# A layer norm, a Hedgehog attention and a SwiGLU on one core: fourteen more matmul instructions for the same columns

## The chip, the cores and the metric

The kernel runs on 1 core of one Trainium2 chip. The metric is the device time of one execution in microseconds (us); where several runs are shown, their median counts. A profile of one execution comes with the runs. Its span is the time from the first to the last instruction of the program; the time of that execution is a little longer than its span.

## The reference, cut to what matters

```python
x = A_x                                   # 1 x 2048 x 640, bf16
xn = _layernorm(x, axis=-1)
return x + _A_ref(xn, A_wqkv, A_w_phi, A_wo) + _B_ref(xn, B_w1, B_w3, B_w2)

def _A_ref(x, wqkv, w_phi, wo):           # 32 heads of 20
    q, k, v = ...                         # x @ wqkv
    phi_q = concat(softmax(q @ w_phi), softmax(-(q @ w_phi)))
    phi_k = concat(softmax(k @ w_phi), softmax(-(k @ w_phi)))
    kv, z = phi_k.T @ v, phi_k.sum(s)
    return ((phi_q @ kv) / (phi_q @ z + 1e-6)) @ wo

def _B_ref(x, w1, w3, w2):                # F = 1536
    return (silu(x @ w1) * (x @ w3)) @ w2
```

## The kernel before

The 2048 tokens are 16 tiles of 128. The order of the work is written out by hand, engine by engine; no planner moves anything, and each engine runs its own list in order. SyncE (SP in the profile) issues all DMAs from one queue.

**Start.** The first tiles of x and parts of the weights are loaded. Until they are there, TensorE multiplies zeros into a bank of PSUM that nobody reads: `warm(n, cols)` (L219 to L221) issues n such idle matmuls of `cols` columns. At the start stand two matmuls of 128 columns and `warm(2 * WARM, P // 2)`, 40 of 64 columns (L223 to L226). Then TensorE transposes tile 0 of x (`by_pe`, L294), runs `warm(4)` (four idle matmuls of 128 columns, L766), and transposes tile 1. Layer norm statistics, V products of the raw tiles (`raw_part`, L306), further transposes by DMA (`by_dma`, L758) and the first SwiGLU units (`glu_half`, L473) follow. The loads of the SwiGLU weights w1 and w3 stand in the same SP queue as the transposes.

**K stage.** For each tile: the fused K projection (`phi_unit`, L411), softmax features, the running sum of phi_k times v (`kv_unit`, L496), and SwiGLU units as filler.

**Q stage** (the loop at L935). For each of the 16 tiles t: the fused Q projection, its softmax features, a transpose of them by DMA, two tiles later the attention product (`r_unit`, L530) and the transpose of its result. For t from 0 to 6 two SwiGLU units fill TensorE: a unit (`glu_unit`, L454; `fill`, L706) has five matmuls of 512 columns for the gate and five for the up product, one for each 128 rows of the weights. `fill_halves(gate, up)` (L710) is the same unit with the last `gate` and `up` of the five matmuls cut into two matmuls of 256 columns with the same weights. Before, at t = 0, it is called as `fill_halves(2, 2)`; all other units are whole. Later turns of the loop compute the output: three groups of four tiles transposed (`out_piece`, L646) and four tiles directly (`out_unit`, L590).

**End.** The last tile's result is computed in three parts of 384, 160 and 96 columns; the first two parts are added and the first is stored. Then every engine comes to a branch (L998): a flag computed on the way says whether the fast softmax without maximum was safe. Where it was not, a general path repeats everything in loops (two loops, 86 matmuls in their bodies). Where it was, as with these inputs, every engine jumps over the general path's code to a short part in which VectorE adds the last 96 columns and SP stores the rest of the tile. On TensorE this code that is jumped over has 335 instructions in the assembled program; nothing is left for TensorE behind it but the closing barrier (L1048). Every matmul of the program is two TensorE instructions, a weight load (PEld) and the product (PE).

```python
        finish = res
        with tc.If(ok == 0) as general:
            ...
        with general.Else():
            nc.vector.memset(drift[:, 0:1], 0.0)
            finish()
```

Of the kernel before, what the change touches and what calls it, by code (L numbers as in the profile page):

```python
# [8 lines left out]
P = 128  # L9
# [3 lines left out]
def kernel(  # L13
# [53 lines left out]
    def bank(name, dt=f32):  # L67
        n = 512 if dt == f32 else 1024
        return psum.tile([P, n], dt, name=name, tag="bank")
# [75 lines left out]
    def ld(dst, src):  # L145
        nc.sync.dma_start(out=dst, in_=src)
# [9 lines left out]
    with tc.manual_schedule():  # L156
# [62 lines left out]
        def warm(n, cols=P):  # L219
            for _ in range(n):  # L220
                nc.tensor.matmul(idle[:, 0:cols], nought[:], nought[:, 0:cols])  # L221
# [19 lines left out]
        def ln_stats(*ts):  # L241
            made = []
            for t in ts:
                xt = xin[:, (t // 4) % 3, t % 4, :]
                st = work.tile([P, 2, 6], f32, name="st")
                for i in range(2):
                    nc.vector.bn_stats(out=st[:, i, :], in_=xt[:, i * HD : (i + 1) * HD])  # L247
                made.append(st)
            for t, st in zip(ts, made):
                nc.vector.bn_aggr(out=mv[:, t, :], in_=st[:])  # L250
# [43 lines left out]
        def by_pe(dst, t, ps):  # L294
            xt = xin[:, (t // 4) % 3, t % 4, :]
            for c in range(KD):
                nc.tensor.transpose(  # L297
                    ps[:, c * P : (c + 1) * P], xt[:, c * P : (c + 1) * P], ident[:]
                )
            for c0, c1 in ((0, 2), (2, KD)):  # L300
                nc.scalar.copy(  # L301
                    out=dst[:, c0:c1, t * P : (t + 1) * P],
                    in_=ps[:, c0 * P : c1 * P].rearrange("p (c s) -> p c s", s=P),
                )
# [43 lines left out]
        def tile_of(t):  # L348
            return slice(t * P, (t + 1) * P)
# [61 lines left out]
        def phi_unit(t, w, name, exps=exps, cols=None):  # L411

            ps = by_token(cols or tile_of(t), w, name, CH)
            dst = phi[:, t % 4]
            exps(ps, dst)
            rows = dst.rearrange("p c g f -> p (c g) f")[:, :, 0:60].rearrange(
                "p a (i d) -> p a i d", d=Dh
            )
            sk = work.tile([P, 2 * NCH, 3], f32, name="sk")
            nc.vector.reduce_sum(out=sk[:], in_=rows, axis=AX.X)  # L420
            rk = work.tile([P, 2 * NCH, 3], f32, name="rk")
            nc.vector.reciprocal(out=rk[:], in_=sk[:])  # L422
            nc.gpsimd.tensor_mul(  # L423
                out=rows, in0=rows, in1=rk[:, :, :, None].to_broadcast([P, 2 * NCH, 3, Dh])
            )
# [28 lines left out]
        def glu_unit(sc, fi, banks=None):  # L454

            gp, up = banks or (bank("gp")[:], bank("up")[:])
            for ps, w in ((gp, w1), (up, w3)):
                for c in range(KD):
                    nc.tensor.matmul(  # L459
                        ps,  # L460
                        w[:, c, fi * P : (fi + 1) * P],
                        xnT[:, c, sc * 512 : (sc + 1) * 512],
                        start=(c == 0),
                        stop=(c == KD - 1),
                    )
            return glu_done(sc, fi, gp, up)

        def glu_done(sc, fi, gp, up):
            th = work.tile([P, 512], f32, name="th")
            nc.scalar.activation(out=th[:], in_=gp, func=AF.Tanh, scale=0.5)  # L470
            return lambda: glu_product(sc, fi, gp, up, th)
# [24 lines left out]
        def kv_unit(t, v1, acc, first, last):  # L496

            for c in range(NCH):
                b, i = divmod(c, 6)
                nc.tensor.matmul(  # L500
                    acc[:, b, VC * i : VC * i + 1 + Dh * HC[c]],
                    phi[:, t % 4, c].rearrange("p g f -> p (g f)"),
                    v1[:, c, 0 : 1 + Dh * HC[c]],
                    start=(first and i == 0),
                    stop=last,
                    skip_group_check=True,
                )
# [77 lines left out]
        def residual(rows):  # L585
            xr = work.tile([P, D], bf, name="xr")
            ld(xr[:], x2[rows, :])
            return xr
# [83 lines left out]
        def group_stored(g, i):  # L672
            rows = out2[(4 * g + 2 * i) * P : (4 * g + 2 * i + 2) * P, :]
            ld(
                rows.rearrange("(t p) d -> p t d", p=P),
                y[:, 2 * i : 2 * i + 2].rearrange("p t c s -> p t (c s)"),
            )
# [28 lines left out]
        def fill(n):  # L706
            for _ in range(n):
                glu_unit(*glu.pop(0))()

        def fill_halves(gate, up):  # L710

            sc, fi = glu.pop(0)
            gp, upp = bank("gp")[:], bank("up")[:]
            for ps, w, whole in ((gp, w1, KD - gate), (upp, w3, KD - up)):
                for c in range(KD):
                    n = 1 if c < whole else 2
                    for i in range(n):
                        a, b = i * 512 // n, (i + 1) * 512 // n
                        nc.tensor.matmul(
                            ps[:, a:b],  # L720
                            w[:, c, fi * P : (fi + 1) * P],
                            xnT[:, c, sc * 512 + a : sc * 512 + b],
                            start=(c == 0),
                            stop=(c == KD - 1),
                            skip_group_check=True,
                        )
            glu_done(sc, fi, gp, upp)()
# [35 lines left out]

        pst = [bank("pst", bf), bank("pst", bf)]
        by_pe(xrT, 0, pst[0])
        warm(4)  # L766
        ln_stats(0)
        ln_root(0)
        by_pe(xrT, 1, pst[1])
# [165 lines left out]
        for t in range(NST + 4):  # L935
            if t < NST:
                phi_unit(t, wqphi, "pq")
            if t < 2:
                kv_unit(turns[t - 2], vaug[:, turns[t - 2]], acc, False, t == 1)
                if t == 1:  # L940
                    kv_done([acc[:, 0], acc[:, 1]])
                    ld(w2, B_w2.rearrange("(c p) d -> p c d", p=P))
            if t < 7:
                (fill_halves(2, 2) if t == 0 else fill(1))
                fill(1)
            for g, c in pieces.get(t, []):
                out_piece(g, c)
            outs = {16: (12,), 19: (13, 14, 15)}.get(t, ())
            for j in outs:
                last = tile_of(j) if j == NST - 1 else None  # L950
                res = out_unit(hT[:, j], tile_of(j % 4), xrs[j], last)
                if j == 13:
                    group_stored(2, 0)
                    group_stored(2, 1)
                if 13 <= j < 15:
                    xrs[j + 1] = residual(tile_of(j + 1))
                if last is None:
                    ld(out2[tile_of(j), :], res[:])
            if 2 <= t < NST + 2:
                r_unit(t - 2)  # L960
            if t < NST:
                phi_transposed(t)
            if 2 <= t < NST + 2:
                o_transposed(t - 2, (t - 2) // 4)
            if t in backs:
                group_back(*backs[t])
            if t in (12, 13):
                group_stored(0, t - 12)
            if t == 17:
                group_stored(1, 0)  # L970
            if 2 <= t < 6:
                x_back(t - 2)
            if 7 <= t < 11:
                x_back(t - 3)
            if 13 <= t < 17:
                x_back(t - 5)
            if t == 15:
                xrs[12] = residual(tile_of(12))
            if t == 17:
                xrs[13] = residual(tile_of(13))  # L980
            if t == 18:
                group_stored(1, 1)
                group_back(2, 0)
                group_back(2, 1)
            if t < 4:
                norm_unit(wqphi, 1, t)
            if t == 4:
                ld(listed[:], norms[:])
                ld(flat, listed[:].rearrange("p g -> (p g)").partition_broadcast(1))
            if t == 10:  # L990
                flag_unit()
            if t == 12:
                ok = nc.values_load(flag[0:1, 0:1], min_val=0, max_val=1)
# [59 lines left out]
```

## Time and profile before

| what | value |
|---|---|
| runs shown | 268.24, 268.84, 269.27 us; median 268.84 |
| the profiled execution's own time | 268.56 us |
| its span | 266.9 us |
| TensorE (PE) busy | 261.0 us, 98% of the span, 1854 matmuls recorded |
| weight loads (PEld) recorded | 1880 |
| VectorE, ScalarE, GpSimd busy | 72%, 42%, 34% |
| DMA | 31.41 MB, 118 GB/s in the mean |

The profile's page lists busy time by engine, the span in 40 slices, DMA queues, the chain of work that ended last, and the costliest groups of instructions; other views of the same trace answer for a window, a line or an engine. A small share of matmul records is missing from a trace: 26 of 1880 here, as each weight load has one matmul. An engine's name with a q (PEldq, SPq) is its sequencer: it waits, branches or issues DMAs, and is not counted as busy. The DMA queues named "instruction" carry the program's code to the engines.

### The profile page before, as it was taken

How to read it: one execution, taken by the hardware profiler on the slowest of the kernel's cores; microseconds unless marked ns; L12 is line 12 of the kernel's file. 1: busy time of each engine (PE TensorE's matmuls, PEld its weight loads, DVE VectorE, ACT ScalarE, POOL GpSimd, SP SyncE). 2: the span in 40 equal slices, each digit the busy share in tenths (PEclk: the TensorE clock that was granted, in tenths of full speed). 3: DMA queues.
4: the chain of work that ended last, by engine and by line, in shares of the span. 5: the costliest groups of instructions: out<-in, count | busy, mean ns of one | idle time of the engine just before them, and what ended most of it. 6: DMA issues, size and time to landing. Idle time of an engine off the chain costs nothing.

```text
span 266.9 us, 5027 instructions
## 1 busy us (share of the span) xinstructions
PE 261.0 (98%) x1854; PEld 153.2 (57%) x1880; DVE 193.3 (72%) x356; ACT 113.0 (42%) x347; POOL 90.7 (34%) x83
## 2 busy tenths in 40 slices
PE   8999999999999999999999999999999999999994
PEld 7766475655556555555655555555555555644663
DVE  4899973397876877799888999999699866125121
ACT  5764344746567753366766554423322330000000
POOL 5022620055544444443373333336434543000000
PEclk9999999999999999999999999999999999999999
DMA  6997866976000001500008855563768789552871
GB/s 190 234 259 168 119 122 144 366 133 122 1 2 0 1 3 8 167 2 0 2 0 251 180 120 116 93 133 89 130 153 97 165 200 159 128 116 47 221 209 55
DMA packets 83484, 31.41 MB, mean 118 GB/s; under 512 B 71935, under 2 KB 82047, under 8 KB 83456
## 3 DMA queue, kind: packets, MB, share of 16 engines
q1 hardware_dynamic: 83456, 31.05, 53.5%
q8 instruction: 16, 0.26, 0.4%
q14 instruction: 12, 0.10, 0.1%
HBM read 11.17 MB, written 2.63 MB: 52 GB/s over the span
## 4 chain that ended last, share of the span: by engine, by line
PE 94%; DMA 2%; ACT 1%; issue 1%; SPq 0%; DVE 0%
PE up L459 18%; PE gp L459 18%; PE acc L652 15%; PE pq L357 8%; PE pk L357 8%; PE acc L598 7%; PE pv L357 6%; PE acc L657 6%; DMA w<-in_B_w_dram 2%; PE pr L535 2%; PE pkv L500 2%; PE pf L443 1%; PE idle L221 1%; PE pst L297 1%; ACT xnT L301 0%
## 5 line engine op out<-in xcount | busy, mean ns | idle before, releaser
L423 POOL TENSOR_TENSOR phi<-phi,rk 128x1320 bf16<-128x1320 bf16 x32 | 77.2, 2414 | 108.9 <-DVE rk L422 86.3
L459 PEld LDWEIGHTS <-w 128*128 128x128 bf16 x450 | 42.6, 98 | 47.4 <-DMA w<-in_B_w_dram 0.7
L420 DVE TENSOR_REDUCE sk<-phi 128x66 f32<-128x1320 bf16 x32 | 48.8, 1525 | 19.6 <-ACT phi L386 18.2
L459 PE MATMUL up<-xnT,w 128*128 128x512 bf16 x224 | 55.9, 379 | 0.2
L459 PE MATMUL gp<-xnT,w 128*128 128x512 bf16 x207 | 54.6, 379 | 1.1 <-DMA w<-in_B_w_dram 0.3
L357 PEld LDWEIGHTS <-xnT 128*128 128x128 bf16 x450 | 42.8, 98 | 19.2
L386 ACT ACTIVATE phi<-pq 128x360 bf16<-128x360 f32 (+2 forms) x96 | 24.8, 364 | 42.1 <-issue 31.8
L652 PE MATMUL acc<-reg_h,reg_v 128*128 128x512 bf16 x180 | 41.3, 379 | 0.0
L470 ACT ACTIVATE th<-gp 128x512 f32<-128x512 f32 x48 | 29.2, 610 | 27.0 <-PE gp L459 27.0
L490 DVE SCALAR_TENSOR_TENSOR reg_h<-gs,up 128x512 bf16<-128x512 bf16 x48 | 33.0, 688 | 5.4 <-PE pv L357 0.5
L487 DVE SCALAR_TENSOR_TENSOR gs<-th,gp 128x512 bf16<-128x512 f32 x48 | 31.4, 654 | 4.8 <-ACT th L470 4.8
L386 ACT ACTIVATE phi<-pk 128x360 bf16<-128x360 f32 (+2 forms) x96 | 24.9, 368 | 19.3 <-PE pk L357 19.3
L652 PEld LDWEIGHTS <-reg_v 128*128 128x128 bf16 x180 | 17.4, 98 | 19.1
L357 PE MATMUL pk<-wkphi,xnT 128*128 128x360 bf16 (+1 forms) x160 | 24.3, 299 | 0.0
L357 PE MATMUL pq<-wqphi,xnT 128*128 128x360 bf16 (+1 forms) x160 | 24.3, 299 | 0.0
L422 DVE RECIPROCAL rk<-sk 128x66 f32<-128x66 f32 x32 | 18.1, 566 | 3.2
L357 PE MATMUL pv<-reg_w,xnT 128*128 128x360 bf16 (+1 forms) x130 | 18.6, 299 | 0.0
L607 DVE TENSOR_TENSOR res<-acc,xr 128x320 bf16<-128x320 f32 (+3 forms) x9 | 3.8, 451 | 16.6 <-PE acc L598 10.5
L247 DVE BATCH_NORM_STATS2 st<-reg_h 128x6 f32<-128x320 bf16 x32 | 13.4, 477 | 2.1 <-DMA reg_h<-in_A_x_dram 2.1
L372 ACT CAST reg_v<-pv 128x360 bf16<-128x360 f32 (+2 forms) x39 | 10.6, 347 | 9.7 <-PE pv L357 9.7
L556 DVE TENSOR_TENSOR o__77<-pr,den 128x360 bf16<-128x360 f32 (+1 forms) x32 | 14.2, 486 | 0.6
L660 DVE TENSOR_TENSOR w<-acc,v_raw 128x512 bf16<-128x512 f32 x10 | 6.6, 671 | 10.5 <-issue 6.0
(90 smaller groups left out, 210.8 us busy)
## 6 DMA issues: line engine op xcount, KB each, us to landing
w<-in_B_w_dram SPq DMA_DIRECT2D x2, 1280.0 KB, 6.1
reg_h<-in_A_x_dram SPq DMA_DIRECT2D x6, 320.0 KB, 5.1
reg_v<-in_B_w_dram SPq DMA_DIRECT2D x1, 1920.0 KB, 8.8
out_dram<-w SPq DMA_DIRECT2D x6, 320.0 KB, 2.7
w<-in_B_w_dram SPq DMA_DIRECT2D x4, 320.0 KB, 5.8
reg_w<-in_A_wqkv_dram SPq DMA_DIRECT2D x5, 160.0 KB, 3.6
reg_w<-in_A_wo_dram SPq DMA_DIRECT2D x1, 800.0 KB, 7.5
reg_h<-in_A_x_dram SPq DMA_DIRECT2D x4, 160.0 KB, 3.7
```

Source lines behind the costliest of these rows:

```text
L357: nc.tensor.matmul(ps[i][:, 0 : b - a], xnT[:, c, cols], w[:, c, a:b], start=(c == 0), stop=(c == KD - 1), skip_group_check=True,)
L386: nc.scalar.activation(out=dst[:, c0 : c0 + n, g, 0:k], in_=p.rearrange("p (c f) -> p c f", c=n), func=AF.Exp, scale=1.0 - 2.0 * g,)
L420: nc.vector.reduce_sum(out=sk[:], in_=rows, axis=AX.X)
L422: nc.vector.reciprocal(out=rk[:], in_=sk[:])
L423: nc.gpsimd.tensor_mul(out=rows, in0=rows, in1=rk[:, :, :, None].to_broadcast([P, 2 * NCH, 3, Dh]))
L459: nc.tensor.matmul(ps, w[:, c, fi * P : (fi + 1) * P], xnT[:, c, sc * 512 : (sc + 1) * 512], start=(c == 0), stop=(c == KD - 1),)
L470: nc.scalar.activation(out=th[:], in_=gp, func=AF.Tanh, scale=0.5)
L487: nc.vector.scalar_tensor_tensor(out=gs[:], in0=th[:], scalar=1.0, in1=gp, op0=ALU.add, op1=ALU.mult)
L490: nc.vector.scalar_tensor_tensor(out=hT[:, 4 * sc : 4 * sc + 4, fi, :], in0=gs[:].rearrange("p (t s) -> p t s", t=4), scalar=0.5, in1=up.r ...
L598: nc.tensor.matmul(ps[:, 0 : b - a], rows[j][0], rows[j][1][:, a:b], start=(j == 0), stop=(j == len(rows) - 1),)
L652: nc.tensor.matmul(acc4, w2[:, k, cols], hT[:, 4 * g : 4 * g + 4, k, :], start=(k == 0), stop=False,)
L657: nc.tensor.matmul(acc[:], wo[:, k, cols], oTs[g][:, k, :], start=False, stop=(k == KD - 1),)
```

## The change

Two places are changed. Between the transposes of tiles 0 and 1, four idle matmuls of 128 columns become eight of 64. In the first turn of the Q stage the unit that had two and two of its matmuls halved has all ten halved, and in the second turn the first unit, whole before, has two and two halved. TensorE gets 4 + 6 + 4 = 14 more matmuls, each with a weight load, and the number of columns that it multiplies stays the same. All of the additional instructions stand ahead of the branch at L998.

```diff
@@ -763,7 +763,7 @@
         pst = [bank("pst", bf), bank("pst", bf)]
         by_pe(xrT, 0, pst[0])
-        warm(4)
+        warm(8, P // 2)
         ln_stats(0)
         ln_root(0)
         by_pe(xrT, 1, pst[1])
@@ -941,7 +941,7 @@
             if t < 7:
-                (fill_halves(2, 2) if t == 0 else fill(1))
+                fill_halves(5, 5) if t == 0 else fill_halves(2, 2) if t == 1 else fill(1)
                 fill(1)
             for g, c in pieces.get(t, []):
                 out_piece(g, c)
```

## Prediction

> **What bounds the kernel now.** I read the page first: its busy times, the DMA queues and the chain of work that ended last.
>
> ```profile
> span 266.9 us, 5027 instructions
> PE 261.0 (98%) x1854; PEld 153.2 (57%) x1880; DVE 193.3 (72%) x356; ACT 113.0 (42%) x347; POOL 90.7 (34%) x83
> q8 instruction: 16, 0.26, 0.4%
> PE 94%; DMA 2%; ACT 1%; issue 1%; SPq 0%; DVE 0%
> ```
>
> TensorE is the bound: 98% busy and 94% of the chain. The remaining few per cent of the chain lie at its two ends, so I read the view of busy time by stretches and the waits.
>
> ```profile
> 17.00:263.50 246.50, 245.01 (x1698) 140.48 (x1724) 180.82 (x317) 101.17 (x317) 87.09 (x63) 1.00 0.52 111
> PEld L459 <- DMA w<-in_B_w_dram: 0.7, 2, 0.6
> ```
>
> From 17.0 to 263.5 us TensorE shows 245.0 of 246.5 us busy at the full granted clock (1.00), and 26 matmuls lack a record (1698 against 1724 weight loads); so it never waits there. Nothing that other engines gain can shorten this stretch. The one wait of any size stands ahead of it, for a load of SwiGLU weights. What is left is the end, in the view of the branch's line and SP's waits in the last 5 us:
>
> ```profile
> L998 PEldq COMPARE_BRANCH  x1: 3244/3244/3244, 262.5 to 262.5; - x1
> L998 SPq COMPARE_BRANCH  x1: 53/53/53, 262.6 to 262.6; - x1
> L998 PEldq EVENT_SEMAPHORE  x1: 51/51/51, 265.9 to 265.9; - x1
> SPq L1048 <- PEq L998: 1.1, 1, 1.1
> ```
>
> The same branch takes SP 53 ns, but TensorE 3244 ns, from 262.5 to 265.8, though its last matmul ends at 263.5. SP's closing barrier waits 1.1 us for it. So the kernel ends with TensorE's branch, not with its work. Code arrives while it waits, as the DMA view of 262.5 to 265 us and then of the last microsecond shows, each with one packet of TensorE's code queue:
>
> ```profile
> q8 instruction: 1, 0.02, 2.6%
> ...
> q8 instruction: 1, 0.02, 6.6%
> ```
>
> The page counts 16 such packets of 0.26 MB in all, 16 KB each. At 64 bytes for an instruction (the assembled program's size over its count) that is 256 instructions, or 128 matmuls with their weight loads. The stretches between packets bear it out. In the view of busy time by stretches these rows run from one packet's start to the next, the last one to the branch (length, TensorE busy, matmuls in brackets, clock, DMA):
>
> ```profile
> 188.10:206.00 17.90, 17.79 (x131) 1.00 0.63 125
> 206.00:223.50 17.50, 17.45 (x126) 1.00 0.99 189
> 223.50:242.30 18.80, 18.69 (x118) 1.00 0.57 108
> 242.30:262.50 20.20, 20.15 (x134) 1.00 0.62 162
> ```
>
> One packet comes every 118 to 131 recorded matmuls. By 262.5 there were 134 since the last: the next packet was due just then. I read it as the ordinary packet, requested a few instructions ahead of the branch, which carries the code to which the branch jumps (335 instructions on). The branch waits for its arrival.
>
> **The change part by part.** It adds 14 matmuls with their weight loads, 28 instructions, ahead of the branch: 8 near 4 us, the other 20 in two units around 134 us.
>
> *Idle matmuls.* From the chain of waits:
>
> ```profile
> 1.21 2.15 PE idle L221 x40
> 3.90 0.43 PE idle L221 x4
> 133.57 1.09 PE gp L719 x7
> 134.66 1.08 PE up L719 x7
> 135.75 1.08 PE gp L459 x5
> ```
>
> Forty of 64 columns take 2.15 us, 54 ns each; eight take 0.43 us, as the four of 128 do. Cost 0, and the start of tile 1's transposes stays.
>
> *Halves.* The halved unit of before shows 7 matmuls in 1.09 and 1.08 us; a whole group of 5 takes 1.08 us right behind them. Two cuts thus cost 0 to 0.01 us. The fully halved units at the start say the same:
>
> ```profile
> 14.46 0.71 PE L476 MATMUL gp<-xnT,w 128*128 128x256 bf16 x5
> 15.00 0.71 PE L476 MATMUL up<-xnT,w 128*128 128x256 bf16 x5
> 15.55 0.71 PE L476 MATMUL gp<-xnT,w 128*128 128x256 bf16 x5
> ```
>
> Five halves start every 0.545 us, 109 ns each, against half of 1.08 us: at most 0.005 us for 2.5 cuts. Ten cuts cost 0.00 to 0.05 us; I take 0.03, all on TensorE's path. The weight load of a half is hidden at 109 ns as it is here. ScalarE and VectorE receive the same tiles at the same times; SP, DVE, ACT and POOL run the same instructions.
>
> *The code packets.* Every packet from then on is requested 14 matmuls earlier in the work, the last one too. How much time that is follows from the last matmuls:
>
> ```profile
> 258.66 2.11 PE L598 MATMUL acc<-reg_v,reg_h 128*128 128x384 bf16 x12
> 260.61 0.98 PE L598 MATMUL acc<-reg_w,reg_v 128*128 128x384 bf16 x5
> 261.42 0.99 PE L598 MATMUL acc<-reg_v,reg_h 128*128 128x160 bf16 x12
> 262.25 0.51 PE L598 MATMUL acc<-reg_w,reg_v 128*128 128x160 bf16 x5
> 262.60 0.67 PE L598 MATMUL acc<-reg_v,reg_h 128*128 128x96 bf16 x12
> 263.11 0.38 PE L598 MATMUL acc<-reg_w,reg_v 128*128 128x96 bf16 x5
> ```
>
> By their starts those of 384 columns take 162 ns (1.95 us for 12), those of 160 take 69, those of 96 take 42. Fourteen matmuls are 0.6 us at the least and 2.3 us at the most. The branch should then end at 263.5 to 265.2 instead of 265.8.
>
> What is late next is the last store:
>
> ```profile
> L146 SPq DMA_DIRECT2D out_dram<-res x2: 332/337/342, 262.2 to 263.8; - x2
> out_dram<-res SPq DMA_DIRECT2D x1, 96.0 KB, 3.3
> out_dram<-res SPq DMA_DIRECT2D x1, 64.0 KB, 1.8
> out_dram<-res SPq DMA_DIRECT2D x1, 160.0 KB, 1.8
> ```
>
> The last one (64 KB) is issued at 263.8 and lands 1.8 us later, at 265.6: with the branch out of the way SP goes on at 265.6 instead of 265.9, a gain of 0.3 us. The one before (96 KB, issued at 262.2) needs 3.3 us where the larger one of 160 KB needs 1.8; the code packet crosses it. If that packet goes ahead of it, the stores may land 0.3 us earlier (an estimate: a sixth of 1.8), and the gain is 0.6 us. I take 0.5, nearer the upper end because the packet then comes at 261 to 262.7 and no longer lies among the stores. Bounds of this term: 0 and 0.6.
>
> [...]
>
> **Sum.** 0 + 0.03 - 0.5 = -0.47 us on the profiled execution: 268.56 to 268.1. That execution is 0.28 us under the median of the runs shown (268.84), so for the median: 268.84 - 0.47 = **268.4 us**.
>
> **Rivals.**
>
> *The fetch is the branch's own.* Then 3.24 us stay whatever stands ahead: 268.84 + 0.03 = 268.9. For it: the packet falls into the branch's 3.2 us. Against it: the count of 134 matmuls, by which an ordinary packet was due. This is also the case in which the change does nothing.
>
> *More is gained.* At the start a code packet falls into 10.5 to 13 us, and the DMA view there shows:
>
> ```profile
> GB/s 291 217 238 291 270 311 553 274 279 266 176 98 49 33 49 41 41 45 33 41 45 41 53 49 41 33 33 25 29 29 25 33 25 33 131 254 452 336 369 430
> q8 instruction: 1, 0.02, 2.3%
> ...
> 11.29 5.75 DMA w<-in_B_w_dram
> ```
>
> Each number is 62 ns: for about 1.4 us, from 11.2 to 12.6, the queues move some 40 instead of 280 GB/s, beside the packet. The chain's last row is the load for which TensorE waits until 17.1. Eight instructions earlier, the packet could miss the transposes that stand in the queue there; TensorE's wait goes from 16.64 (15.55 and two groups of 0.545) to 17.10, so 0.46 us are to be had: 267.9. And if the 1.66 us around the span hold the packet that still travels at its end (6.6% of 16 engines for 1 us is 1.06 us), up to 0.7 us more: 267.2. Against both: no row ties the hold or that time to the packet.
>
> *Slower.* The same place, the other way: a packet that comes at a worse moment among the transposes holds the queues as long again, 1.4 us, and the load that follows comes 1.4 us later. TensorE waits for this load already, so the price counts in full from the first 0.01 us: 268.4 + 1.4 = 269.8, and 270.3 without the gain at the end. In the Q stage such a hold costs nothing up to the slack that keeps TensorE free of waits. Against it: the packet moves by only four matmuls.
>
> **How the numbers follow.** Chances: forecast 0.54, the branch's own fetch 0.15, more gained 0.19, slower 0.12. A change of over 0.5% (1.34 us, about what a measurement of this kernel can tell from none) is under 267.5 or over 270.2. Under it lie the far half of the second rival and a remainder for what I don't see: 0.16. Over it lies the worse form of the third: 0.10. Within: 0.74. The range of 267.3 to 269.5 reaches from nearly the whole second rival to 0.6 us beyond the first, for the scatter of the runs shown (268.24 to 269.27), and leaves 0.07 below and 0.13 above.
>
> **What would show it.** In the changed profile TensorE's branch at L998 should take 0.9 to 2.7 us instead of 3.24, its code packet should come before 262.8, SP's wait for TensorE at L1048 should be gone or under 0.3 us, and the span should be 266.3 to 266.6. The ten halves of the first Q turn should start every 109 ns, eight idle matmuls should take 0.43 us. A branch of still 3.2 us shows the first rival. A wait for w at 17.1 that is gone or has grown shows the second or third. A wait of TensorE between 17 and 263 us would prove me wrong on the whole.

## The result and the profile after

The change is slower by 0.4%: 269.14 us median (268.34 to 269.76, 22 runs) against 268.06 (267.20 to 269.63, 22 runs), ratio 1.0041, 95% interval [1.0030, 1.0051]. The prediction was 268.4 us, for a gain of 0.47 us. The profiled execution took 269.05 us with a span of 267.2 us (before: 268.56 and 266.9).

The view of TensorE's branch after the change, with count, length (least, median, most, in ns) and start:

```profile
L998 PEldq COMPARE_BRANCH  x1: 775/775/775, 262.4 to 262.4; - x1
L998 PEldq EVENT_SEMAPHORE  x1: 51/51/51, 263.4 to 263.4; - x1
```

The branch takes 0.78 us instead of 3.24, a little less than the 0.9 to 2.7 us that the prediction named. The next view is SP's waits in the last 5 us of the changed kernel (engine and line, what it waited for, us in total, times, longest):

```profile
SPq L146 <- DVE res L607: 2.8, 2, 1.6
SPq L1048 <- DMA out_dram<-res: 1.6, 1, 1.6
SPq L1048 <- PEq L1048: 0.6, 2, 0.5
```

The wait for TensorE (1.1 us before) is gone, and in its place stands a wait of 1.6 us for the last store (the 0.6 us for L1048 are the closing barrier's own and stand in every run). The DMA view of the changed kernel gives the time from issue to landing of the last two stores:

```profile
out_dram<-res SPq DMA_DIRECT2D x1, 96.0 KB, 1.6
out_dram<-res SPq DMA_DIRECT2D x1, 64.0 KB, 2.7
```

Before, the 96 KB took 3.3 us and the 64 KB took 1.8. The trouble has moved from the last store but one, which had time to spare, to the last, which ends the kernel. The trace has 16 landings for each store. Of the last one, 15 come within 1.83 us of VectorE's last addition (263.38) in the changed kernel, just as before; the sixteenth comes at 2.97. The DMA view of 263.8 to 264.0 us names what comes in between:

```profile
q8 instruction: 1, 0.02, 42.2%
```

It is a packet of TensorE's code that starts at 263.92 and travels for 1.35 us, while the store's data begins to move at 264.5. It is not the packet for which the branch waits (that one starts at 260.60, 1.8 us ahead of the branch) but the one behind it. It starts 0.74 us after TensorE has landed behind its branch. Before, the same packet started at 266.53, when everything was stored. The DMA view of 263 to 266 us shows what it does to the store (each number is 75 ns):

```profile
GB/s 338 328 226 103 0 0 0 109 0 0 0 0 218 0 0 0 0 0 0 0 171 287 239 116 7 0 0 0 0 0 14 7 7 7 0 20 0 0 0 0
```

The 218 at 263.9 is the code packet. Of the store's 128 packets of 512 bytes, 120 start from 264.50 to 264.85. Then nothing starts until 265.26, when the last eight follow, and the code packet's record ends at 265.27 (263.92 and 1.35).

The added work is as cheap as predicted. From the timeline of TensorE in the changed kernel (start, us, what):

```profile
133.25 1.25 PE L719 MATMUL gp<-xnT,w 128*128 128x256 bf16 x10
134.34 1.25 PE L719 MATMUL up<-xnT,w 128*128 128x256 bf16 x10
135.44 1.24 PE L459 MATMUL gp<-xnT,w 128*128 128x512 bf16 x4
```

Ten halves start 1.09 us after the ten before them, 109 ns each. From 17 to 263.5 us TensorE shows no gap but the missing records and one wait of about 0.28 us at 38 us (two matmuls of L357 start 430 ns apart there instead of 152; they wait for a transposed tile of x, where the two kernels have the same code). From the first of these halves to VectorE's last addition it is 130.12 us in both profiles of the change, against 130.10 in both of before. The last addition itself starts at 263.38 and 262.78 us, against 263.52 and 263.13 before. So none of the loss lies ahead of it.

### The profile page after: what moved, and what is told of

Same layout as the page of the kernel before. It is cut to its first block, busy times and chain, and to the rows that moved or that the text cites. A ratio compares the mean times of both kernels' runs of the same rounds, so it can differ in the third digit from the quotient of the medians.

```text
span 267.2 us, 5055 instructions
## 1 busy us (share of the span) xinstructions
PE 260.9 (98%) x1868; PEld 154.3 (58%) x1894; DVE 193.2 (72%) x356; ACT 113.0 (42%) x347; POOL 90.7 (34%) x83
## 4 chain that ended last, share of the span: by engine, by line
PE 86%; DVE 8%; DMA 2%; issue 1%; POOL 1%; SPq 0%; ACT 0%; DVEq 0%
PE up L459 16%; PE gp L459 15%; PE acc L652 15%; PE pq L357 8%; PE pk L357 8%; PE acc L598 7%; PE acc L657 6%; DVE st L247 3%; PE pv L357 2%; PE pr L535 2%; PE pkv L500 2%; DVE reg_h L490 2%; DVE reg_h L289 1%; DVE gs L487 1%; DMA reg_w<-in_A_wqkv_dram 1%
## 5 line engine op out<-in xcount | busy, mean ns | idle before, releaser
L459 PEld LDWEIGHTS <-w 128*128 128x128 bf16 x440 | 41.7, 98 | 45.8
L459 PE MATMUL up<-xnT,w 128*128 128x512 bf16 x219 | 54.6, 379 | 0.2
L459 PE MATMUL gp<-xnT,w 128*128 128x512 bf16 x202 | 53.3, 379 | 0.9
L357 PEld LDWEIGHTS <-xnT 128*128 128x128 bf16 x450 | 42.7, 98 | 19.6 <-DMA xnT<-reg_h 0.5
L357 PE MATMUL pk<-wkphi,xnT 128*128 128x360 bf16 (+1 forms) x160 | 24.3, 299 | 0.0
L357 PE MATMUL pq<-wqphi,xnT 128*128 128x360 bf16 (+1 forms) x160 | 24.3, 299 | 0.0
L357 PE MATMUL pv<-reg_w,xnT 128*128 128x360 bf16 (+1 forms) x130 | 18.8, 299 | 0.1
L607 DVE TENSOR_TENSOR res<-acc,xr 128x320 bf16<-128x320 f32 (+3 forms) x9 | 3.8, 451 | 16.2 <-PE acc L598 10.5
```

Source lines behind the costliest of these rows:

```text
L357: nc.tensor.matmul(ps[i][:, 0 : b - a], xnT[:, c, cols], w[:, c, a:b], start=(c == 0), stop=(c == KD - 1), skip_group_check=True,)
L459: nc.tensor.matmul(ps, w[:, c, fi * P : (fi + 1) * P], xnT[:, c, sc * 512 : (sc + 1) * 512], start=(c == 0), stop=(c == KD - 1),)
```

## The experiments

Two numbers are read off every trace: when the code packet behind the branch's own starts, and when the span ends, both counted from VectorE's last addition (L607, 96 columns). The second leaves out whatever happens earlier in the execution. "Instructions" is what TensorE has more than before ahead of the branch. A last landing is called late by its distance from the fifteenth. The theories are numbered in the expectation of e1.

| run | instructions | branch, us | packet starts | store's 15th, last landing | span's end | median us | ratio to before |
|---|---|---|---|---|---|---|---|
| before, first profile | 0 | 3.24 | +3.01 | 1.83, 2.12 | 3.34 | 268.06 | 1 |
| before_again | 0 | 2.82 | +2.58 | 1.79, 1.82 | 2.92 | one run | |
| e3_change_net0 | 0 | 3.40 | +3.16 | 1.82, 2.28 | 3.49 | 268.64 | 1.0022 [1.0010, 1.0035] |
| e2_idle_only | 8 | 2.58 | +2.36 | 1.79, 1.83 | 2.72 | 267.70 | 0.9991 [0.9977, 1.0004] |
| e2_again | 8 | 2.84 | +2.59 | 1.79, 1.83 | 2.93 | 267.59 | 0.9994 [0.9973, 1.0016] |
| e5_n8_by_halves | 8 | 2.74 | +2.50 | 1.79, 1.82 | 2.83 | 267.86 | 0.9996 [0.9982, 1.0010] |
| e1_halves_only | 20 | 1.64 | +1.39 | 1.82, 3.99 | 4.88 | 269.10 | 1.0022 [1.0004, 1.0041] |
| e1_again | 20 | 1.50 | +1.47 | 1.82, 3.51 | 4.41 | one run | |
| the change | 28 | 0.78 | +0.54 | 1.83, 2.97 | 3.87 | 269.14 | 1.0041 [1.0030, 1.0051] |
| after_again | 28 | 1.36 | +1.13 | 1.82, 3.71 | 4.60 | one run | |
| e4_more_halves | 40 | 0.48 | +0.32 | 1.82, 2.68 | 3.57 | 268.33 | 1.0016 [1.0004, 1.0028] |
| e6_n60_by_halves | 60 | 0.38 | +0.17 | 1.83, 2.20 | 3.10 | 268.41 | 1.0012 [0.9992, 1.0033] |
| e7_change_tail20 | 68 | 0.48 | +1.40 | 1.82, 3.41 | 4.30 | 269.49 | 1.0054 [1.0034, 1.0075] |
| e8_change_tail38 | 104 | 0.48 | +1.64 | 1.79, 1.83 | 2.73 | 267.75 | 0.9979 [0.9962, 0.9995] |

In the first profile of before and in e3 the last landing is 0.3 and 0.5 us late though the packet comes only at +3. There the branch's own packet, at -0.18 and -0.29, travels until +0.84 and +1.00, and the last packets of the 96 KB store start only as it ends (from +0.83 and +0.99), ahead of the last store's.

**e1: the halves alone** (`warm(4)` as before).

```diff
-                (fill_halves(2, 2) if t == 0 else fill(1))
+                fill_halves(5, 5) if t == 0 else fill_halves(2, 2) if t == 1 else fill(1)
```

> Only the halves of the change: 20 more TensorE instructions ahead of the branch, the idle matmuls as before. Theory 1 (the place of the branch in TensorE's 256-instruction code packets decides; the packet after the branch's own is requested 0.7 us after TensorE resumes and holds up one of the 16 landings of the last store if it comes between 263.5 and 265.5 us): the branch ends near 264.7, its stall is about 2.2 us, the next packet starts near 265.4 and misses the last store, so this run is 0.2 to 0.6 us FASTER than before. Theory 2 (the halves and idle matmuls themselves cost time): slower by 20/28 of the change's 1.1 us, about 0.8 us. Theory 3 (the first code packet, moved by the idle matmuls, disturbs the first loads): as before, within 0.2 us.

The runs lie in two groups, 267.7 to 268.0 (four) and 269.1 to 269.8 (six). SP's waits in the profile, which is of the upper group:

```profile
SPq L146 <- DVE res L607: 3.4, 2, 2.2
SPq L1048 <- DMA out_dram<-res: 2.7, 1, 2.7
SPq L1048 <- PEq L1048: 0.6, 2, 0.5
```

I had expected it to be faster, and it was slower: TensorE's jump ended at 263.8 us and not at 264.7 as I had worked out, and the packet came at 264.5 (+1.39), into the store's data (+1.1 to +1.5). The last landing is 2.2 us late. The theory's mechanism stands; the time at which it put the packet (265.4) was wrong.

> The halves alone once more, for a second profile: its runs lie in two groups, 267.7 to 268.0 and 269.1 to 269.8 us. Theory 1: in the lower group the code packet starts late enough to miss one landing of the last store (span's end about 3 us behind the last product's start), in the upper it holds it back (5.1 us). Which of the two this run falls into is open.

It fell into the upper group once more. That the lower group are executions in which the packet came behind the data is thus argued, not shown: no profile is of that group.

**e2: the idle matmuls alone** (`warm(8, P // 2)`, halves as before).

> Only the idle matmuls of the change: 8 more TensorE instructions, all units as before. Theory 1: the branch's packet comes 0.3 us earlier, the stall is about 3 us, the end moves by 0 to 0.3 us to the fast side; the first packet moves by 8 instructions, which may shift the wait for the first weights by up to 0.5 us either way. Theory 2: slower by about 0.3 us. Theory 3: slower by the whole 1.1 us.

```profile
SPq L146 <- DVE res L607: 3.4, 2, 2.2
SPq L1048 <- PEq L1048: 0.6, 2, 0.5
SPq L1048 <- PEq L998: 0.5, 1, 0.5
```

Here, in SP's waits, TensorE holds SP for 0.5 us and the store does not at all: the packet comes at +2.36. As theory 1 said, and against theories 2 and 3.

> The idle matmuls alone once more, for the interval: 0.1 to 0.5 us under before, span's end 2.9 to 3.1 us behind the last product's start; the version to keep if theory 1 holds.

The span's end was as expected (2.93), the interval holds no change too.

**e3: the whole change with 14 idle matmuls fewer at the very start.**

```diff
-        warm(2 * WARM, P // 2)
+        warm(25, 98)
+        warm(1, 110)
```

> The whole change, with 14 fewer idle matmuls at the very start for the same 2560 idle columns (26 of 98 or 110 for 40 of 64), so that the branch stands at the same instruction number as before. Theory 1: branch stall 3.2 us again, last store undisturbed as before, time within 0.3 us of before. Theory 2: as slow as the change, about 1.1 us. Theory 3: undecided, the first packet comes 20 instructions later than before.

The end is that of before, branch and all (3.49). The time is not: 268.64 us against 267.97 is more than the 0.3 us that theory 1 allowed. From the first half to the last addition it is 130.12 us as in the change, so the loss lies ahead of that. The profiled execution, with 269.47 us the slowest of the eleven, shows it in the waits of TensorE around 17 us:

```profile
PEld L460 <- DMA w<-in_B_w_dram: 2.1, 1, 2.1
PE up L460 <- DMA w<-in_B_w_dram: 1.6, 1, 1.6
```

This wait for the SwiGLU weights (lines are one further down here) has nothing to do with the end. It is 0.46 us in the first profile of before, none in both of the change, and 1.4 us in e5, whose start is that of before to the instruction. So it scatters from one execution to the next by more than the change is worth, and whether e3's start makes it longer is left open.

**e4: the change, and all ten halved in the second turn too** (`fill_halves(5, 5) if t < 2 else fill(1)`).

> The change, and the first unit of the second turn halved throughout as well: 40 more TensorE instructions than before. Theory 1: the branch's packet starts near 259.5, the branch does not stall (under 0.2 us), the next packet starts near 263.3 and is through before the last store's data moves at 264.5, so the last store lands as early as it can: 0.3 to 0.8 us FASTER than before, about 1.5 us faster than the change. Theory 2: slower than the change, 1.4 to 1.6 us over before. Theory 3: as the change, 1.1 us over before.

A miss: the branch costs 0.48 us though its packet started 2.5 us ahead of it, so the packet behind it came at +0.32 and not before 0. The store's last landing was 0.86 us late. The run is slower than before, but by less than the change, though six more matmuls are cut; theory 2 has it the other way.

**e5: eight instructions by halves** (`fill_halves(4, 4) if t == 0 else fill(1)`, `warm(4)`).

> 8 more TensorE instructions ahead of the branch, this time by four more halves in the first unit of the Q stage and none among the idle matmuls. Theory 1, mended (what counts is when the code packet behind the branch's own starts: ahead of or among the last store's data, 1.3 to 2.0 us behind the start of the last matmul, it holds one of that store's 16 landings back by 0.8 to 2 us; later it does no harm): as the run with 8 more idle-matmul instructions, branch stall near 2.6 us, next packet 2.5 us behind the last matmul's start, the span ends 2.9 to 3.1 us behind it, time 0 to 0.4 us under before. Theory 2 (halves cost time): slower than before by 0.3 us or more. Theory 3 (the idle matmuls at the start decide): as before.

The end, 2.83, lies between those of e2's two profiles (2.72 and 2.93) with other instructions: the count matters here, not the kind.

**e6: sixty instructions** (`fill_halves(5, 5) if t < 3 else fill(1)`, `warm(8, P // 2)`).

> The change, and the first units of the second and third turn halved throughout: 60 more TensorE instructions than before, 26 more halves. Theory 1, mended: the branch's packet is there in time, no stall; the next packet starts 0.0 to 0.3 us behind the start of the last matmul and is through by 1.4 us, as the last store's data starts: its last landing is at most 0.4 us behind the others, the span ends 2.9 to 3.4 us behind the last matmul, time 0.5 to 1.2 us under the change's. Theory 2: over 1.5 us slower than before, slower than the change. Theory 3: as the change.

The packet at +0.17, the last landing 0.37 us late, the end at 3.10: as expected. From the first half to the last addition it is 130.16 us, so 26 more matmuls than before cost 0.06 us in the units (theory 2 asked for over 1.5 us).

**The two kernels once more.**

> The kernel before, for a second profile. Theory 1: branch stall of 3.2 to 3.4 us, code packet behind it over 3 us behind the last matmul's start, span's end 3.5 to 3.8 us behind it. The wait for the first SwiGLU weights near 17 us is expected to differ from the first profile's (0.46 us), as the runs of before spread by over 1 us.

> The changed kernel, for a second profile. Theory 1: branch stall near 0.8 us, next code packet 0.7 to 0.9 us behind the last matmul's start, the last store's last landing about 1.1 us behind its other 15, span's end 4.0 to 4.3 us behind the last matmul. Theories 2 and 3: the end as in before, and waits or longer matmuls elsewhere, at the halves or ahead of 20 us.

Of before, the branch took 2.82 us, less than expected, and SP went on when TensorE did (end 2.92, also under the expected 3.5 to 3.8). The ends of e2 and e5 can't be told from this one, so eight more instructions neither gain nor lose anything that these runs show. Of the change, the branch took 1.36 us instead of some 0.8, and the packet came later, at +1.13, which is worse: SP's waits show

```profile
SPq L1048 <- DMA out_dram<-res: 2.4, 1, 2.4
SPq L146 <- DVE res L607: 1.1, 1, 1.1
SPq L1048 <- PEq L1048: 0.6, 2, 0.5
```

**e7 and e8: the change, with TensorE kept busy behind its last product.** Nobody waits for these idle matmuls; they only delay TensorE's jump.

```diff
                 ok = nc.values_load(flag[0:1, 0:1], min_val=0, max_val=1)
+        idle = bank("idle")
+        warm(20, P // 2)
```

> The change, and 20 idle matmuls of 64 columns on TensorE between its last product and the branch, for which nobody waits. They delay TensorE's jump by 20 x 54 = 1.1 us. Theory 1, mended: the jump ends about 0.7 us behind the start of the last product, the next code packet starts about 1.5 us behind it, in the midst of the last store's data: the store's last landing is 1.5 to 2.2 us behind the others in most executions, span's end 4.4 to 5.2 us behind the last product's start, time 0 to 1 us over the change's. Rival (the code packet has nothing to do with the late landing; the change's end is slow for another reason, its halves or its instruction count): end as in the change, 4.1 to 4.9 us.

> The change, and 38 such idle matmuls between the last product and the branch, a delay of TensorE's jump by 2.05 us. Theory 1, mended: the next code packet starts about 2.5 us behind the last product's start, behind the last store's data, whose 16 landings come together; span's end 2.9 to 3.2 us behind the last product's start; FASTER than the change by 1.0 to 1.5 us though TensorE has 2 us more work at its end. Rival: no faster than the change.

These two runs decide. SP's waits of e7, then of e8:

```profile
SPq L146 <- DVE res L607: 2.6, 2, 1.5
SPq L1050 <- DMA out_dram<-res: 2.1, 1, 2.1
SPq L1050 <- PEq L1050: 0.6, 2, 0.5
```

```profile
SPq L146 <- DVE res L607: 3.4, 2, 2.2
SPq L1050 <- PEq L1050: 0.6, 2, 0.5
SPq L1050 <- DMA out_dram<-res: 0.5, 1, 0.5
```

The packet among the store's data in e7 (DMA view of 264.5 to 265 us, each number 12.5 ns, the packet is the 1434), and alone behind them in e8 (264.8 to 265 us, each number 5 ns):

```profile
GB/s 164 164 123 83 1434 41 82 0 41 0 0 0 0 0 0 0 0 0 0 0 0 0 0 0 0 0 0 0 0 0 0 0 0 0 0 0 0 0 0 0
GB/s 0 0 0 0 0 0 0 0 0 0 0 0 0 0 0 0 3277 0 0 0 0 0 0 0 0 0 0 0 0 0 0 0 0 0 0 0 0 0 0 0
```

And the timeline of TensorE at the end of e8:

```profile
262.82 0.38 PE L598 MATMUL acc<-reg_w,reg_v 128*128 128x96 bf16 x5
263.04 1.27 PE L221 MATMUL idle<-nought 128*128 128x64 bf16 x38
```

With 20 the packet falls into the store (+1.40), and the kernel is as slow as the change (0.35 us slower by the medians, but the intervals overlap); with 38, 0.24 us further on (+1.64), it misses it: the fifteenth landing is at +1.79 and the last at +1.83, SP's 0.5 us for the store are its ordinary travel (1.5 us from issue to landing, as in before_again), and the kernel is 1.39 us faster than the change by the medians (269.14 to 267.75; before, run beside each, had 268.06 and 268.07). The delay was smaller than I had said, 1.27 us for 38, 33 ns each (I had used the 54 ns that one takes at the start), but enough. e8 beats both kernels: against before 0.9979, interval [0.9962, 0.9995].

## Why the prediction was wrong, point by point

The measured 269.14 us lies within the stated range of 267.3 to 269.5, but by luck: the forecast started from the median of three runs, 268.84, where 22 runs of before have 268.06. The forecast gain of 0.47 us is a loss of 1.08.

- **What bounds the kernel**: right. From the first matmul of the unit with the halves to the last addition it is 130.10 to 130.16 us in all 14 profiles, and the end decided. The prediction would have had a wait between 17 and 263 us prove it wrong on the whole; the wait of 0.28 us at 38 us in the first profile of the change is such a wait, but the second profile, equally slow, has none.
- **Idle matmuls and halves**: right. The eight idle matmuls start 0.45 us ahead of tile 1's transposes, the four of before 0.43; the ten halves start 109 ns apart. The cuts cost 0.02 us in the change, where the prediction had 0.03, and 0.06 in e6 for 26.
- **The branch's packet**: right. It is the ordinary packet: from the first of the 16 to the fifteenth the view of busy time by stretches counts 1774 weight loads in before and 1744 in the change, 127 and 125 for each packet, with their matmuls some 250 instructions. In the runs, 20, 28, 40 and 60 more instructions move it from 0.2 us ahead of the last addition (first profile of before) to 1.9, 2.8, 3.5 and 4.0 us ahead, and the branch falls from 3.24 us to 0.38. It scatters, too: the second profiles of before, of 20 and of 28 more have 0.7, 2.1 and 2.0. In the ten profiles in which the branch takes over 0.5 us it ends 2.35 to 2.72 us behind this packet's start. In before the packet starts 0.79 and 0.24 us behind the branch's own start, so those profiles alone could not tell it from a fetch that the branch starts. That reading is ruled out by the changed profile, where the packet starts 1.8 us ahead of the branch. What code the packet carries, no view shows.
- **"What is late next is the last store", landing at 265.6 or earlier**: this is the step that failed. The prediction took the store's landing as fixed once the branch is out of the way, even as improved ("no longer lies among the stores"). But behind TensorE's branch one more code packet comes: in all 14 profiles it starts behind the branch's end, by 0.72 to 0.82 us in twelve, by 0.95 and 1.05 us in e1_again and e7, where it comes among the store's data. Freeing the branch early sent that packet into the last store (+0.54 us instead of +3.01). The predicted gain of 0.5 us became a loss of 0.5 (3.87 against 3.34) to 1.7 us (4.60 against 2.92) at the end; the means of the two profiles each, 4.24 and 3.13, differ by 1.1 us like the medians, but two profiles each are few.
- The packet stood in the prediction's own rows: 6.6% of the last microsecond of before. I used it only as a price in a rival ("the 1.66 us around the span"), and did not ask when it would come if TensorE came earlier. In the traces the packet moves with the jump: it starts at +3.01 in the first profile of before, behind a branch of 3.24 us, and at +0.54 in that of the change, behind one of 0.78 us.
- **The rivals**: "slower" was there with the wrong place. The wait for w at 17 us is gone in both profiles of the change, which the prediction named as a sign of the second or third rival; but it is gone in both of e1 too, which starts like before, and over all profiles it varies between 0 and 1.8 us without order. So no run ties the start to the change. The time around the span stayed between 1.66 and 1.88 us in the 22 runs of the change, so nothing was gained there either.

## What to carry to other kernels

Where a program ends behind a branch, look at the code packets in its last microseconds: here the packet behind a branch of 0.78 us started at +0.54 instead of the +3.01 behind one of 3.24 us, and the last store's last landing came at 2.97 us instead of 2.12. A wait at the end that goes away must be followed by the question what the freed engine does next, DMAs of its own code included. Compare ends by a mark near the end (here the last addition), because a start that scatters as here (0 to 1.8 us in the wait for w at 17 us) hides a difference of 0.5 us in the total.

## What the runs showed that I had not expected

- A 16 KB code packet, whose own travel is 0.93 to 1.52 us here, held back one of a store's 16 landings: by 0.4 us when it started at +0.17, 0.9 at +0.32, 1.1 at +0.54, 1.9 at +1.13 and 1.6 to 2.2 at +1.39 to +1.47; at +1.64 by nothing. The data of the undisturbed store moves until +1.47.
- In both profiles of the change and of e1, in e4 and in e7, 120 of the store's 128 packets start by +1.47, and the first of the last eight starts 0.01 to 0.02 us ahead of the end of the code packet's record; in e8 all 128 start by +1.47. The trace does not name the DMA engines, so that these eight and the code packet share one is inferred from this. What holds the eight until the packet's record begins, in e1_again at +1.47, when all other data has moved, stays open.
- TensorE's taken branch took 0.48 us in e4 and 0.38 in e6, though its packet started 2.5 us or more ahead of it there, against 0.05 us on SP.
- 38 idle matmuls on TensorE behind its last product, 1.27 us of them, made the kernel 1.4 us faster than the change.
